# Folding w3 into w_out: multiplying each piece one step behind its transposes, and handing the steps out singly

## The chip, the cores and the metric

The kernel runs on one core of a Trainium2 chip. The metric is the device time of one execution in microseconds (us); of several runs the median counts. TensorE is PE in the profile (its weight loads PEld), VectorE is DVE, ScalarE is ACT, GpSimd is POOL, and SyncE, whose queue issues the DMAs, is SP.

## What is computed

```python
x = attention(q, k, v, M_prev, z_prev, beta)      # 2304 tokens x 512
h = x @ w_in                                      # 512 -> 2048
x2 = (h * tanh(softplus(h))) @ w_out              # 2048 -> 512
a, b = x2 @ w1, x2 @ w2                           # 512 -> 1024
out = ((a * b) @ w3) @ w_out2                     # 1024 -> 1024 -> 512
```

The inputs are 64-bit floats. The kernel decodes the weights from pairs of 32-bit words on the chip and multiplies in three terms (high x high, high x low, low x high). As nothing stands between the last two products, it computes W = w3 @ w_out2 once (the fold), and then out = (a * b) @ W.

## The kernel before

There are three stages in one program. **Stage one** is the attention (up to some 500 us). **Stage two** is the first feed-forward net. It goes through the quarters g = 0..3 of its 2048 hidden columns, and in each through eight units (b, z) of 288 tokens. `emit_h(u)` (L454) makes the hidden block: four PSUM tiles of 12 matmuls each, then tanh and friends on ScalarE and the splitting into gh and gl. `emit_x2(u)` (L560) multiplies it back and adds into x2 (L577, VectorE), in four rows of 12 matmuls; it is emitted one unit behind. **Stage three** (from L662) goes through 40 work items k = (c, m): five spans c of up to 512 tokens, eight blocks m of 128 hidden columns. `emit_ab(k)` (L699) makes two products of 12 matmuls and their product a * b, split into a ring of six; `emit_out(k - 5)` (L717) multiplies with W, five items behind.

**The fold** is a generator, `fold()` (L579), beside stage two's last quarter. It loads o2 (the split w_out2, 4 MB) into the memory that quarter 2's weights leave. Then, for each of the eight row blocks m and four column pieces g, a step loads 128 x 256 values of w3 (L92), decodes them (L98 to L104 on VectorE, L105 on GpSimd), transposes them in two halves into a PSUM tile (L597), copies the high part w3h out (L599, ScalarE), subtracts for the low part w3l (L600, by the helper of L65, VectorE), and multiplies: six matmuls into the accumulator `po`. After four pieces the row block leaves in two halves: ScalarE copy, VectorE subtraction, a store of 256 KB to w_dram (L611 to L613), with one buffer `wo`. There are 32 steps.

Five steps at a time are drawn in each unit of the last quarter but the first, between `emit_h` and `emit_x2` (L644, L645); the calls in stage three (L739, L674) only take what is left, which is nothing by then. W is loaded back (`wft`) in `end_fold()` (L673), called after the fifth work item.

PSUM has eight banks in three groups: A (3), X (3) and F (2). In the last quarter `emit_h` takes three A and one X, `emit_x2` takes X, and F belongs to the fold, one bank for `po` and one for the transposed piece. In stage three the second product of every odd work item takes F, and so does the fourth output tile of a span.

The order on each engine isn't the order of the text: a planner (the option `schedule_with_timeline_sim`) goes through the program on times that it works out itself, and gives each engine the earliest-written instruction that is ready by these times and whose tile has a free buffer. The order that comes out is fixed; on the chip the engines only wait for each other's semaphores. All DMAs of this part are issued from SP.

Of the kernel before, what the change touches and what calls it, by code (L numbers as in the profile page):

```python
# [21 lines left out]
def fused_kernel(ctx: ExitStack, tc, q, k, v, M_prev, z_prev, beta, w_in, w_out, w1, w2, w3, w_out2, out):  # L22
# [29 lines left out]
    def psF():  # L52
        return bank("F")

    def f(ap):
        return ap.bitcast(F32)
# [51 lines left out]
    def words(w, r0, c0):  # L108
        return w[r0:r0 + 128, c0:c0 + dec["w"]].bitcast(I32)
# [341 lines left out]
    HU = {(0, 0, 0): "AXAX", (0, 0, 1): "FXFX"}  # L451
    gt = {}

    def emit_h(u):  # L454

        g, b, z = u
        t = wts[g]
        x = xl[b]
        cs = slice(CH * z, CH * z + CH)
        y = [wps[0].tile([128, 2, CH], F32, tag=f"y{i}", name="y", bufs=1) for i in range(2)]  # L460
        hp = []
        for m in range(KQ):
            o = bank(HU.get(u, HT[g == NQ - 1])[m])[:, 0:CH]
            ms = slice(128 * m, 128 * m + 128)
            for kk in range(KD):
                mm(o, t[:, 0, kk, ms], x[:, 0, kk, cs], kk == 0, False)
                mm(o, t[:, 0, kk, ms], x[:, 1, kk, cs], False, False)
                mm(o, t[:, 1, kk, ms], x[:, 0, kk, cs], False, kk == KD - 1)
            hp.append(o)
        for m in range(KQ):  # L470
            nc.scalar.activation(out=y[m // 2][:, m % 2], in_=hp[m], func=AF.Tanh, scale=0.5)

        d = wps[0].tile([128, 1], F32, tag="dum", name="dum", bufs=2)
        first = nc.scalar.activation(out=d, in_=y[1][:, 1, 0:1], func=AF.Sin, scale=0.0)
        with tc.issue_after(first.ins):
            for i in range(2):
                nc.scalar.activation(out=y[i], in_=y[i], func=AF.Arctan, scale=-0.5, bias=half)
        gg = []
        for i in range(2):
            nc.scalar.activation(out=y[i], in_=y[i], func=AF.Sin, scale=-2.0, bias=halfpi)  # L480
            for j in range(2):
                nc.vector.tensor_tensor(out=y[i][:, j], in0=y[i][:, j], in1=hp[2 * i + j], op=ALU.mult)  # L482
            gh = wps[0].tile([128, 2, CH], F32R, tag="gh", name="gh", bufs=3)
            gl = wps[0].tile([128, 2, CH], F32R, tag="gl", name="gl", bufs=3)
            nc.scalar.copy(out=gh, in_=y[i])  # L485
            sub(gl, y[i], gh)
            gg.append((gh, gl))
        gt[u] = gg
# [68 lines left out]
    fk = ExitStack()  # L557
    fpool = [None]

    def emit_x2(u):  # L560
        g, b, z = u
        t = wts[g]
        gg = gt.pop(u)
        c0 = S * b + CH * z
        for m in range(KD):
            o = psX()[:, 0:CH]
            ms = slice(128 * m, 128 * m + 128)
            for kk in range(KQ):
                gh, gl = (x[:, kk % 2] for x in gg[kk // 2])
                mm(o, t[:, 0, KD + kk, ms], gh, kk == 0, False)  # L570
                mm(o, t[:, 1, KD + kk, ms], gh, False, False)
                mm(o, t[:, 0, KD + kk, ms], gl, False, kk == KQ - 1)
            d = x2[:, m, c0:c0 + CH]
            if g == 0:
                nc.vector.tensor_copy(out=d, in_=o)  # L575
            else:
                nc.vector.tensor_tensor(out=d, in0=d, in1=o, op=ALU.add)  # L577

    def fold():  # L579
        o2 = wq.tile([128, 2, 8, DM], F32R, tag="wq0", name="o2")  # L580
        oh, ol = o2[:, 0], o2[:, 1]
        for h in range(2):
            for i in range(2):
                dm(
                    out=f(o2[:, i, 4 * h:4 * h + 4]),
                    in_=o2_dram[i, 512 * h:512 * h + 512].rearrange("(k p) f -> p k f", p=128),
                )
        for m in range(FF2 // 128):
            po = psF()
            fp = fpool[0]  # L590
            for g in range(4):
                a, e = decode(words(w3, 128 * m, 256 * g))
                th = fp.tile([128, 2, 128], F32R, tag="w3h", name="w3h", bufs=2)
                tl = fp.tile([128, 2, 128], F32R, tag="w3l", name="w3l", bufs=2)
                pt = psF()[:, 0:256]
                for j in range(2):
                    nc.tensor.transpose(pt[:, 128 * j:128 * j + 128], a[:, 128 * j:128 * j + 128], ident)  # L597
                pw = pt.rearrange("p (a b) -> p a b", b=128)
                nc.scalar.copy(out=th, in_=pw)  # L599
                sub(tl, pw, th)  # L600
                for j in range(2):
                    kk = 2 * g + j
                    mm(po, th[:, j], oh[:, kk], kk == 0, False)
                    mm(po, th[:, j], ol[:, kk], False, False)
                    mm(po, tl[:, j], oh[:, kk], False, kk == 7)
                if g < 3:
                    yield
            for h in range(2):
                cs = slice(256 * h, 256 * h + 256)
                wo = fp.tile([128, 2, 256], F32R, tag="wo", name="wo", bufs=1)  # L610
                nc.scalar.copy(out=wo[:, 0], in_=po[:, cs])  # L611
                sub(wo[:, 1], po[:, cs], wo[:, 0])
                dm(out=w_dram[:, 128 * m:128 * m + 128, cs].rearrange("i p c -> p i c"), in_=f(wo))  # L613
            yield

    def from_dram(t, d, cols):
# [4 lines left out]
        return xp.tile([128, 2, KD, 512], F32R, tag=f"xs{s}", name=name, padded_shape=[128, 2, KD, S])  # L621

    folding = fold()
    nextq = iter(())
    prev = None
    w1t, w2t = [None, None], [None, None]
    for u in [(g, b, z) for g in range(NQ) for b in range(B) for z in range(2)]:
        g, b, z = u
        last = g == NQ - 1
        if u not in gt:  # L630
            if last and fpool[0] is None:
                steps(nextq, 100)
                steps(pre, 100)
                dk.close()
                fpool[0] = fk.enter_context(tc.tile_pool(name="fp", bufs=1))
                decoder(fk, 3, 2, 256)
            emit_h(u)
        if last:
            if z == 0 and b > 0:
                wt, wd = ((w1t, w1_dram), (w2t, w2_dram))[(b - 1) % 2]  # L640
                i = (b - 1) // 2
                wt[i] = w_slot(b - 1, "w12t")
                from_dram(wt[i], wd, slice(512 * i, 512 * i + 512))
            if (b, z) > (0, 0):  # L644
                steps(folding, 5)  # L645
        if prev is not None:
            emit_x2(prev)
        if not last:
            if b == 0 and z == 0:
                nextq = load_quarter(g + 1)  # L650
            steps(nextq, 2)
            steps(pre, 1)
        prev = u
    emit_x2(prev)
    w2t[1] = w_slot(3, "w12t")
    from_dram(w2t[1], w2_dram, slice(512, 1024))
    wk.close()
# [3 lines left out]

    wp3 = ctx.enter_context(tc.tile_pool(name="wp3", bufs=1, side="right"))  # L662
    T = 512
    NM = FF2 // 128
    RING = 6
    wft = [None]

    room = w2q[0].tile([128, 2 * RING + KD, T], F32R, tag="wq1", name="room")
    ring = room[:, 0:2 * RING].rearrange("p (r i) t -> p r i t", i=2)

    xs_ = {0: (wp3.tile([128, KD, T], F32R, name="x2h"), room[:, 2 * RING:])}

    def end_fold():  # L673
        steps(folding, 100)  # L674
        fk.close()
        late = ctx.enter_context(tc.tile_pool(name="late", bufs=1))
        x = late.tile([128, 2, KD, T], F32R, name="x2s")
        xs_[1] = (x[:, 0], x[:, 1])
        wft[0] = wq.tile([128, 2, NM, DM], F32R, tag="wq0", name="wft")
        for s in range(2):  # L680
            for i in range(2):
                dm(
                    out=f(wft[0][:, i, 4 * s:4 * s + 4]),
                    in_=w_dram[i, 512 * s:512 * s + 512, :].rearrange("(k p) f -> p k f", p=128),
                )

    spans = [(t, min(T, NT - t)) for t in range(0, NT, T)]
    work = [(c, m) for c in range(len(spans)) for m in range(NM)]
# [28 lines left out]
    def emit_out(k):  # L717

        c, m = work[k]
        t0, n = spans[c]  # L720
        t = ring[:, k % RING]
        if m == 0:
            outs[c] = [bank(tag) for tag in "XXXF"[0:n // 128]]
        for i, o in enumerate(outs[c]):
            ts = slice(128 * i, 128 * i + 128)
            mm(o, t[:, 0, ts], wft[0][:, 0, m], m == 0, False)
            mm(o, t[:, 0, ts], wft[0][:, 1, m], False, False)
            mm(o, t[:, 1, ts], wft[0][:, 0, m], False, m == NM - 1)
            if m == NM - 1:
                ob = wp3.tile([128, DM], F32, tag="ob", name="ob", bufs=2)  # L730
                nc.scalar.copy(out=ob, in_=o)
                dm(out=out[t0 + 128 * i:t0 + 128 * i + 128, :], in_=ob)
# [2 lines left out]
    split_x2(0)  # L735
    for k, (c, m) in enumerate(work):
        emit_ab(k)
        if k < LAG:
            steps(folding, 1)  # L739
        if k == LAG - 1:  # L740
            end_fold()
        if m == 5 and c + 1 < len(spans):
            split_x2(c + 1)
        if k >= LAG:
            emit_out(k - LAG)
# [34 lines left out]
```

## Time and profile before

| | us |
|---|---|
| median of 3 runs | 1074.87 (1072.59 to 1078.11) |
| profiled execution | 1077.63 |
| its span, first to last instruction | 1075.8 |
| PE busy | 1018.0 (95%) |
| VectorE busy | 678.0 (63%) |
| ScalarE busy | 540.9 (50%) |
| GpSimd busy | 392.7 (37%) |
| mean granted PE clock | 0.989 |

All times within the execution are us from the start of its span. A group of instructions is named by its line, engine, operation, output and inputs. Idle time stands with what ended it. A matmul's slice overlaps the next one's, and its end is modelled, so that starts say more than lengths.

### The profile page before, as it was taken

How to read it: one execution, taken by the hardware profiler on the slowest of the kernel's cores; microseconds unless marked ns; L12 is line 12 of the kernel's file. 1: busy time of each engine (PE TensorE's matmuls, PEld its weight loads, DVE VectorE, ACT ScalarE, POOL GpSimd, SP SyncE). 2: the span in 40 equal slices, each digit the busy share in tenths (PEclk: the TensorE clock that was granted, in tenths of full speed). 3: DMA queues.
4: the chain of work that ended last, by engine and by line, in shares of the span. 5: the costliest groups of instructions: out<-in, count | busy, mean ns of one | idle time of the engine just before them, and what ended most of it. 6: DMA issues, size and time to landing. Idle time of an engine off the chain costs nothing.

```text
span 1075.8 us, 17622 instructions
## 1 busy us (share of the span) xinstructions
PE 1018.0 (95%) x6360; PEld 874.8 (81%) x6360; DVE 678.0 (63%) x1630; ACT 540.9 (50%) x1128; POOL 392.7 (37%) x393
## 2 busy tenths in 40 slices
PE   6898898889998999999999999999889999999998
PEld 5665656567798999999999999998668888888897
DVE  6599999896689788988887456666543212121111
ACT  5675767577766566666666565643132122221212
POOL 7568898784255456555655011111100000000000
PEclk9999999999999999999999999999999999999999
DMA  6688777775233343334332174334232010100101
GB/s 148 166 188 190 179 185 177 168 187 124 79 88 99 108 143 133 104 120 150 111 106 98 51 274 149 124 94 144 68 121 76 1 40 1 40 1 1 40 1 59
DMA packets 115687, 116.60 MB, mean 108 GB/s; under 512 B 71952, under 2 KB 78096, under 8 KB 115600
## 3 DMA queue, kind: packets, MB, share of 16 engines
q1 hardware_dynamic: 115600, 115.48, 37.8%
q8 instruction: 50, 0.82, 0.3%
q14 instruction: 37, 0.30, 0.1%
HBM read 71.83 MB, written 21.50 MB: 87 GB/s over the span
## 4 chain that ended last, share of the span: by engine, by line
PE 61%; DVE 18%; DMA 7%; POOL 7%; issue 4%; SPq 1%; ACT 1%; DVEq 0%; POOLq 0%; ACTq 0%
PE psA L59 23%; PE psX L59 21%; PE psF L59 12%; DVE de L104 3%; POOL da L120 2%; PE psF L426 2%; DVE da L102 2%; DMA w_dram<-da 2%; DVE de L103 2%; POOL da L105 2%; DVE da L99 2%; DVE da L98 2%; DVE s L361 1%; DVE da L100 1%; PE psX L262 1%
## 5 line engine op out<-in xcount | busy, mean ns | idle before, releaser
L105 POOL TENSOR_TENSOR da<-da,de 128x512 f32<-128x512 f32 (+1 forms) x88 | 105.3, 1200 | 315.5 <-DVE de L104 287.9
L59 PE MATMUL psX<-gh,wqt 128*128 128x288 f32 x1024 | 209.8, 298 | 10.6 <-DVE x L575 6.1
L59 PEld LDWEIGHTS psX<-gh,wqt 128*128 128x128 f32 x1024 | 164.6, 188 | 13.9 <-DVE x L575 7.3
L59 PE MATMUL psX<-gl,wqt 128*128 128x288 f32 x512 | 151.5, 296 | 0.0
L59 PE MATMUL psA<-xt,wqt 128*128 128x288 f32 x840 | 122.6, 298 | 0.0
L59 PEld LDWEIGHTS psA<-xt,wqt 128*128 128x128 f32 x840 | 116.5, 191 | 2.2 <-issue 1.0
L366 ACT ACTIVATE s<-s,acc 128x512 f32<-128x512 f32 (+4 forms) x144 | 84.2, 587 | 40.0 <-DVE acc L361 34.3
L98 DVE TENSOR_SCALAR da<-draw 128x512 int32<-128x512 int32 (+1 forms) x88 | 46.6, 532 | 81.8 <-PE psF L597 31.1
L59 PEld LDWEIGHTS psX<-gl,wqt 128*128 128x128 f32 x512 | 96.8, 189 | 0.4
L712 ACT COPY bs<-psA 128x512 f32<-128x512 f32 (+1 forms) x40 | 21.8, 544 | 123.4 <-PE psA L59 118.5
L59 PE MATMUL psX<-wft,room 128*128 128x512 f32 x336 | 82.4, 390 | 0.0
L59 PE MATMUL psA<-x2h,w12t 128*128 128x512 f32 (+1 forms) x288 | 80.2, 355 | 0.5 <-ACT x2h L696 0.5
L426 PE MATMUL psF<-ident,s 128*128 128x128 f32 x400 | 68.1, 284 | 10.8 <-DVE s L356 7.2
L59 PE MATMUL psF<-xt,wqt 128*128 128x288 f32 x552 | 77.3, 295 | 0.0
L59 PEld LDWEIGHTS psF<-xt,wqt 128*128 128x128 f32 x552 | 74.5, 188 | 0.1
L59 PE MATMUL psX<-pt,raw 128*64 128x64 f32 (+4 forms) x576 | 74.1, 328 | 0.0
L361 DVE CUSTOM_DVE_ANT_0 s<-psA,mask 128x512 f32<-128x512 f32 (+3 forms) x144 | 64.2, 478 | 15.2 <-PE psA L59 11.4
L59 PEld LDWEIGHTS psX<-wft,room 128*128 128x128 f32 x336 | 62.6, 188 | 12.6
L485 ACT CAST gh<-y 128x576 fp32r<-128x576 f32 x64 | 43.2, 675 | 56.0 <-DVE y L482 40.2
L713 DVE TENSOR_TENSOR bs<-bs,psA 128x512 f32<-128x512 f32 (+1 forms) x20 | 12.7, 634 | 93.1 <-PE psA L59 92.4
L428 ACT COPY pt<-psF 128x512 f32<-128x512 f32 (+1 forms) x112 | 57.2, 541 | 26.0 <-PE psF L426 25.7
L426 PEld LDWEIGHTS psF<-ident,s 128*128 128x128 f32 x400 | 48.0, 145 | 27.3 <-issue 7.1
(130 smaller groups left out, 2219.0 us busy)
## 6 DMA issues: line engine op xcount, KB each, us to landing
draw<-in_moe_w_out_dram SPq DMA_DIRECT2D x24, 512.0 KB, 3.7
draw<-in_moe_w_in_dram SPq DMA_DIRECT2D x16, 512.0 KB, 4.4
draw<-in_moe_w_dram SPq DMA_DIRECT2D x16, 512.0 KB, 4.1
draw<-in_moe_w_dram SPq DMA_DIRECT2D x32, 256.0 KB, 3.0
w12t<-w_dram SPq DMA_DIRECT2D x8, 1024.0 KB, 7.3
out_dram<-ob SPq DMA_DIRECT2D x18, 256.0 KB, 2.0
eqk<-hl SPq DMA_DIRECT2D x30, 144.0 KB, 2.6
eqk<-hk SPq DMA_DIRECT2D x30, 144.0 KB, 2.7
```

The costliest lines, as they stand in the source:

```text
L59: nc.tensor.matmul(o, lhsT=l, rhs=r, start=start, stop=stop)
L98: V.tensor_scalar(out=ai, in0=hw, scalar1=0x7FFFFFFF, scalar2=None, op0=ALU.bitwise_and)
L99: V.tensor_scalar(out=a, in0=a, scalar1=2.0 ** -15, scalar2=122879.9921875, op0=ALU.max, op1=ALU.min)
L102: V.scalar_tensor_tensor(out=ai, in0=hw, scalar=-0x40000000, in1=ai, op0=ALU.bitwise_and, op1=ALU.bitwise_or)
L104: V.scalar_tensor_tensor(out=e, in0=lw.bitcast(U32), scalar=2.0 ** -52, in1=e, op0=ALU.mult, op1=ALU.mult)
L105: nc.gpsimd.tensor_tensor(out=a, in0=a, in1=e, op=ALU.add)
L361: nc.vector.tensor_tensor_reduce(out=s, in0=o, in1=m, op0=ALU.add, op1=ALU.min, scale=-scale, scalar=init, accum_out=a,)
L366: nc.scalar.activation(out=s, in_=s, func=AF.Exp, scale=-1.0, bias=a, accum_out=r)
L426: nc.tensor.transpose(o[:, 128 * x:128 * x + 128], src[:, 128 * jb:128 * jb + 128], ident)
L428: nc.scalar.copy(out=t[:, 0:n], in_=o[:, 0:n])
L485: nc.scalar.copy(out=gh, in_=y[i])
L712: nc.scalar.copy(out=bs, in_=pb)
```

## The change

The fold's loop becomes one loop over 33 steps: step s decodes, transposes and splits piece s, and then multiplies piece s - 1, kept in `held`; `po` is taken when the multiplication of a row's first piece is emitted. The steps are drawn one at a time: one after the second of `emit_h`'s four tiles, one after each of `emit_x2`'s four rows, in the same units as before. What `end_fold()` did (drawing the rest, closing the fold's pool, opening the pool with x2s, loading `wft`) stands ahead of the last `emit_x2`, and the calls within stage three go.

```diff
@@ emit_h
+            if m in (1,):
+                steps(beside, 1)
@@ emit_x2
                 nc.vector.tensor_tensor(out=d, in0=d, in1=o, op=ALU.add)
+            steps(beside, 1)
@@ fold
-        for m in range(FF2 // 128):
-            po = psF()
-            fp = fpool[0]
-            for g in range(4):
-                a, e = decode(words(w3, 128 * m, 256 * g))
+        held = None
+        po = None
+        fp = fpool[0]
+        for s in range(4 * (FF2 // 128) + 1):
+            piece = None
+            if s < 4 * (FF2 // 128):
+                a, e = decode(words(w3, 128 * (s // 4), 256 * (s % 4)))
                 ...
                 nc.scalar.copy(out=th, in_=pw)
                 sub(tl, pw, th)
+                piece = (s, th, tl)
+            if held is not None:
+                n, th, tl = held
+                m, g = n // 4, n % 4
+                if g == 0:
+                    po = psF()
                 for j in range(2):
                     kk = 2 * g + j
                     mm(po, th[:, j], oh[:, kk], kk == 0, False)
                     mm(po, th[:, j], ol[:, kk], False, False)
                     mm(po, tl[:, j], oh[:, kk], False, kk == 7)
-                if g < 3:
-                    yield
-            for h in range(2):
-                ...
+                if g == 3:
+                    for h in range(2):
+                        ...
+            held = piece
             yield
@@ stage two
-            emit_h(u)
+            emit_h(u, folding if last and (b, z) > (0, 0) else iter(()))
         ...
-            if (b, z) > (0, 0):
-                steps(folding, 5)
         if prev is not None:
-            emit_x2(prev)
+            emit_x2(prev, folding if last and (b, z) > (0, 0) else pre0)
         ...
-    emit_x2(prev)
+    NM = FF2 // 128
+
+    steps(folding, 100)
+    fk.close()
+    late = ctx.enter_context(tc.tile_pool(name="late", bufs=1))
+    x2s = late.tile([128, 2, KD, 512], F32R, name="x2s")
+    wft = wq.tile([128, 2, NM, DM], F32R, tag="wq0", name="wft")
+    for s in range(2):
+        for i in range(2):
+            dm(
+                out=f(wft[:, i, 4 * s:4 * s + 4]),
+                in_=w_dram[i, 512 * s:512 * s + 512, :].rearrange("(k p) f -> p k f", p=128),
+            )
+    emit_x2(prev, pre0)
     w2t[1] = w_slot(3, "w12t")
     from_dram(w2t[1], w2_dram, slice(512, 1024))
@@ stage three
-    def end_fold():
-        ...
         emit_ab(k)
-        if k < LAG:
-            steps(folding, 1)
-        if k == LAG - 1:
-            end_fold()
```

## Rows read from the trace of the kernel before

**Rows 1.** The page's engine lines: busy us, share of the span, instructions.
```profile
PE 1018.0 (95%) x6360; PEld 874.8 (81%) x6360; DVE 678.0 (63%) x1630; ACT 540.9 (50%) x1128; POOL 392.7 (37%) x393
```

**Rows 2.** Windows: stretch, length, busy us per engine (instructions), granted clock, DMA share, GB/s.
```profile
600.00:620.00 20.00, 19.93 (x139) 19.93 (x140) 9.92 (x26) 11.99 (x19) 1.19 (x2) 0.91 0.08 23
645.27:665.27 20.00, 20.00 (x140) 19.13 (x139) 13.74 (x40) 10.51 (x19) 2.20 (x3) 1.00 0.50 164
745.27:798.74 53.47, 44.96 (x187) 32.98 (x186) 29.75 (x80) 11.16 (x26) 6.84 (x9) 0.97 0.26 79
850.00:1000.00 150.00, 150.00 (x663) 124.24 (x662) 30.23 (x46) 31.75 (x55) 0.00 (x0) 1.00 0.04 16
```

**Rows 3.** Groups of PE by form, 745.5 to 798.7: count, busy us and mean ns, idle before.
```profile
L59 PE MATMUL psF<-o,w3h 128*128 128x512 f32 x44 | 15.5, 435 | 5.6 <-DVE w3l L65 2.8 <-ACT w3h L599 2.8
L59 PE MATMUL psA<-x2h,w12t 128*128 128x512 f32 x48 | 15.4, 396 | 0.5 <-ACT x2h L696 0.5
L59 PE MATMUL psF<-o,w3l 128*128 128x512 f32 x22 | 9.5, 433 | 0.6 <-DVE w3l L65 0.6
L59 PE MATMUL psA<-room,w12t 128*128 128x512 f32 x24 | 9.4, 392 | 0.0
L59 PE MATMUL psF<-x2h,w12t 128*128 128x512 f32 x16 | 5.4, 397 | 0.8 <-DVE bs L713 0.8
L597 PE MATMUL psF<-ident,da 128*128 128x128 f32 x22 | 4.5, 286 | 1.0 <-DVE wo L65 1.0
L59 PE MATMUL psF<-room,w12t 128*128 128x512 f32 x8 | 3.1, 392 | 0.0
```

**Rows 4.** The chain that ended last: start us, us, what (xinstructions).
```profile
745.47 0.63 ACT x2h L696
...
790.54 4.42 PE psF L59 x18
...
853.14 2.72 PE psA L59 x12
```

**Rows 5.** Timeline of PE: start us, us, instruction, count.
```profile
625.29 0.39 PE L59 MATMUL psF<-o,w3h 128*128 128x512 f32 x1
625.52 0.38 PE L597 MATMUL psF<-ident,da 128*128 128x128 f32 x2
...
679.81 0.38 PE L597 MATMUL psF<-ident,da 128*128 128x128 f32 x2
...
683.09 0.63 PE L59 MATMUL psF<-o,w3h 128*128 128x512 f32 x2
...
684.35 0.40 PE L59 MATMUL psF<-o,w3l 128*128 128x512 f32 x1
...
685.27 0.38 PE L597 MATMUL psF<-ident,da 128*128 128x128 f32 x2
685.41 0.38 PE L59 MATMUL psA<-xt,wqt 128*128 128x288 f32 x1
...
690.33 0.38 PE L597 MATMUL psF<-ident,da 128*128 128x128 f32 x2
...
697.39 0.38 PE L597 MATMUL psF<-ident,da 128*128 128x128 f32 x2
...
745.27 0.38 PE L597 MATMUL psF<-ident,da 128*128 128x128 f32 x2
746.14 0.74 PE L59 MATMUL psA<-x2h,w12t 128*128 128x512 f32 x2 [0.49 <-ACT x2h L696]
```

**Rows 6.** Timelines of ACT and DVE: the row leaving behind the transposes at 690.33.
```profile
690.53 0.37 ACT L611 CAST wo<-psF 128x256 fp32r<-128x256 f32 x1 [1.90 <-PE psF L59]
...
695.23 0.42 DVE L65 TENSOR_TENSOR wo<-psF,wo 128x256 fp32r<-128x256 f32 x1 [1.82 <-ACT wo L611]
```

**Rows 7.** Timelines of DVE and PE: a decode that waits, and PE behind it.
```profile
595.70 0.29 DVE L98 TENSOR_SCALAR da<-draw 128x256 int32<-128x256 int32 x1 [6.71 <-DMA draw<-in_moe_w_dram]
...
600.07 0.53 PE L59 MATMUL psX<-gh,wqt 128*128 128x288 f32 x2 [2.29 <-DVE x L577]
```

More of the change, by code (lines that the diff above doesn't have):

```diff
@@ L452, in fused_kernel, with emit_h @@
     gt = {}
-    def emit_h(u):
+    def emit_h(u, beside=iter(())):
         g, b, z = u
@@ L558, in fused_kernel, with emit_x2 @@
     fpool = [None]
-    def emit_x2(u):
+    def emit_x2(u, beside):
         g, b, z = u
@@ L605, in fold @@
                     mm(po, tl[:, j], oh[:, kk], False, kk == 7)
-                if g < 3:
-                    yield
-            for h in range(2):
[L609 to L613, printed above, removed]
+                if g == 3:
+                    for h in range(2):
+                        cs = slice(256 * h, 256 * h + 256)
+                        wo = fp.tile([128, 2, 256], F32R, tag="wo", name="wo", bufs=1)
+                        nc.scalar.copy(out=wo[:, 0], in_=po[:, cs])
+                        sub(wo[:, 1], po[:, cs], wo[:, 0])
+                        dm(out=w_dram[:, 128 * m:128 * m + 128, cs].rearrange("i p c -> p i c"), in_=f(wo))
+            held = piece
             yield
@@ L623, in fused_kernel @@
     folding = fold()
+    pre0 = iter(())
     nextq = iter(())
@@ L663, in fused_kernel @@
     T = 512
-    NM = FF2 // 128
     RING = 6
-    wft = [None]
     room = w2q[0].tile([128, 2 * RING + KD, T], F32R, tag="wq1", name="room")
     ring = room[:, 0:2 * RING].rearrange("p (r i) t -> p r i t", i=2)
-    xs_ = {0: (wp3.tile([128, KD, T], F32R, name="x2h"), room[:, 2 * RING:])}
-    def end_fold():
[L674 to L685, printed above, removed]
+    xs_ = {0: (wp3.tile([128, KD, T], F32R, name="x2h"), room[:, 2 * RING:]), 1: (x2s[:, 0], x2s[:, 1])}
     spans = [(t, min(T, NT - t)) for t in range(0, NT, T)]
@@ L725, in emit_out @@
             ts = slice(128 * i, 128 * i + 128)
-            mm(o, t[:, 0, ts], wft[0][:, 0, m], m == 0, False)
-            mm(o, t[:, 0, ts], wft[0][:, 1, m], False, False)
-            mm(o, t[:, 1, ts], wft[0][:, 0, m], False, m == NM - 1)
+            mm(o, t[:, 0, ts], wft[:, 0, m], m == 0, False)
+            mm(o, t[:, 0, ts], wft[:, 1, m], False, False)
+            mm(o, t[:, 1, ts], wft[:, 0, m], False, m == NM - 1)
             if m == NM - 1:
```

## The prediction

> **What bounds the kernel now.** First the page's engine line: TensorE (PE) is busy 95% of the span [rows 1], so only stretches where it does less can give time back. The windows show where [rows 2]: it is busy for all of 645.27 to 665.27, inside stage two's last quarter, and all of 850 to 1000, inside stage three; the stretch that falls short is 745.27 to 798.74, the seam between them, with 44.96 of 53.47 us. That figure flatters it, since a matmul's slice overlaps the next one's start. I count work instead. The instructions of the seam by form [rows 3] are 66 matmuls of the fold (44 + 22), 96 of stage three (48 + 24 + 16 + 8) and 22 transposes. In steady stage three 12 matmuls of 512 columns take 2.72 us on the chain [rows 4], 0.2267 each; a transpose pair moves the next matmul by 0.14 us (685.27 to 685.41 in the timeline [rows 5]). So the seam holds 162 x 0.2267 + 11 x 0.14 = 38.3 us of work, and **15.2 us of it are empty**, a little of it at the lower clock (granted 0.97 on average [rows 2]).
>
> Two measures of the empty time differ. By matmul slices it is 53.47 - 44.96 = 8.5 us; by count 15.2; by weight loads, busy 32.98 of 53.47 against 124.24 of 150 at full stream [rows 2], it is 53.47 - 32.98 x 150 / 124.24 = 13.7. I take the count. The Trainium skill (Perfetto Trace Analysis, Identifying the Most-Contended Engine) says that matmul busy share is no good measure of the distance to the limit and that the share of LDWEIGHTS is. The trace agrees, 13.7 lying near 15.2; by the slices alone the sum below would end at 1067, not 1061.
>
> Why the seam is empty is in the timeline of PE [rows 5]. A piece's two transposes (L597) are followed by a ScalarE copy, a VectorE subtraction, then six matmuls, and only then by the next piece's transposes: 679.81, matmuls from 683.09, first matmul with w3l at 684.35, next transposes 685.27. From the second piece (625.52) to the 22nd (745.27) there are 20 intervals, 5.99 us each. Inside a row block they are 5.1 to 5.5; each fourth is longer (690.33 to 697.39), because the two F banks hold the accumulator and one transposed piece, and the next piece waits until the finished row is out, through copy, subtraction, store, copy, subtraction (690.53 to 695.65 [rows 6]). F banks are taken in the order of their first write: the second piece's transposes come only behind the first multiplication (625.29, 625.52), which waited for o2. So when stage two ends 10 pairs of transposes and 11 multiplications remain, and the first work item of stage three whose second product goes to F (k = 1) stands behind all of them. Four halves of A work run meanwhile (72 matmuls), then PE has the fold's chain alone; k = 1 ends in the 18 matmuls from 790.54 [rows 4].
>
> **The change part by part.** Nothing is computed less: the same 64 transposes, 192 matmuls, 32 decodes, 32 loads and 16 stores.
>
> 1. *Multiply one step behind.* Transposes of piece s+1 now stand ahead of the six matmuls of piece s. They need the F bank of piece s, free once w3l is subtracted. The interval inside a row, 5.46 and 5.06 us in two cases (679.81, 685.27, 690.33 [rows 5]), loses the six matmuls, 6 x 0.2267 = 1.36 us: 4.1 and 3.7. From above it is bounded by 684.35 - 679.81 = 4.5, when w3l was used at the latest. I take 4.2, nearest to the middle of the three. At a row's end the next accumulator needs the old one's bank, but one more piece is transposed before it is needed. From a row's first transposes: the row before ends 1.5 us later, its bank is out 7 us after that (690.33 to 697.39, the planner's own spacing), one more piece follows at once, so two pieces take 9 us, then two at 4.2, and 1 us for the w3h buffer that waits for the late multiplication: about 18.5 us a row against 24 now.
>
> 2. *Where it ends.* The second piece no longer waits for o2, the third does, so at 625.5 the fold is one piece ahead. It is at the fourth piece near 631, at the fifth near 635, six rows later (6 x 18.5) at 746, and at the last near 760, its subtraction done near 764. Stage two meanwhile takes in the matmuls that stood behind it: 745.27 + 66 x 0.2267 + 11 x 0.14 = 761.8. So fold and stage two end together. If the fold is late, the 72 matmuls that need no F bank cover 16.3 us, until 778. Only a row of 20.5 us or more eats into the gain.
>
> 3. *Steps handed out singly.* No instruction more; it lowers a step's priority against the row blocks of `emit_x2`, and so keeps x2's additions from queueing behind five decodes. Zero, bounds -1 (the stall of [rows 7], gone) to the rival below. VectorE, busy 13.74 of 20 us with four pieces [rows 2], gets five in the 21 us of a longer unit: it covers them.
>
> 4. *W's transfer with the second stage's end.* Four issues on SP, waiting for the fold's last stores and o2's last reader. They start near 768; W is first needed by `emit_out(0)` behind six work items (6 x 24 x 0.2267 = 32.6 us after the start of stage three, near 795). Zero either way. Behind them on SP stands the last quarter of w2, needed by the fifth item, 21.8 us after stage three starts. It is read into a buffer free since the last `emit_h`, so the planner should issue it first; if it does not, it lands some us later and costs 0 to 5. I take 0. The late pool takes the fold pool's memory, as now.
>
> 5. *The seam that stays.* The first matmul of stage three waits for a cast of x2 into memory that stage two's last matmul frees: 745.27 to 746.14 [rows 5], the cast 0.63 [rows 4], so 0.87 us; bounds 0 (a late piece of the fold fills it) and 2.3, the x2 wait of [rows 7].
>
> Sum: four work items (96 x 0.2267 = 21.8 us) end at 761.8 + 0.9 + 21.8 = 784.5, where before it was 798.74. **Gain 14.2 us**, bounds 11 and 15.2; I round to 13.9, for the last unit has a thinner cover. The profiled execution took 1077.63 (span 1075.8): 1063.7 by the sum. The median of the runs shown is 1074.87, 2.8 lower, so I forecast **1061.0**.
>
> **Rivals.** *The interval hardly shrinks.* Decoding, a busy ScalarE or the row-end store sets the pace, say 21.5 us a row: the last transposes come near 635 + 6 x 21.5 + 16 = 780, the F bank 4 us later, some 6 us behind the cover: about 1067 to 1069. For: a row's end already costs 7 us and ScalarE has table loads in its way. Against: inside a row transposes follow the multiplication directly, so the decoded words were there. Chance 0.11.
>
> *Nothing moves.* The planner still puts each multiplication first, because both become ready with the same subtraction, and row ends get no shorter: the fold ends where it did, 1073 to 1076. Against: program order favours the transposes now, and planner and trace follow it for F banks. Chance 0.06.
>
> *VectorE blocks PE.* At 595.70 a decode had waited 6.71 us for its load, x2's addition stood behind it, and PE idled 2.29 us [rows 7]; the 20 us that follow ran at a granted 0.91 [rows 2], another 1.8 us. That is 4.1 us. With five pieces a unit and additions between them it could happen in each of the seven units with steps: 28.7 us; from four on (16.4) it eats the gain, at five or six the kernel takes about 1081. The Trainium skill (PSUM — Partial Sum Buffer, Engine vs sequencer instructions) says that VectorE's queue is strictly first in, first out, which speaks for this rival: a decode that waits holds the additions behind it. The trace shows it that once. Against: in 645.27 to 665.27 PE did not idle with four pieces [rows 2], and the three load buffers stay. Chance 0.07.
>
> **How the numbers follow.** Main case 0.76, first rival 0.11, second 0.06, third 0.07. About 0.5% (5.4 us) is what a measurement of this kernel can tell from no change. Faster by more than that: all of the main case and 0.07 of the first rival, 0.83; within: the rest of it, the second rival and a mild third, 0.11; slower: 0.06. The main case alone spans 1057.5 (gain 15.2, and 2 us by which medians of three differ here) to 1065; with the first rival the range goes to 1069.
>
> **What would show it.** Right: transposes ahead of the previous piece's multiplication, rows of the fold about 18.5 us apart, the last transposes near 760, PE without a hole between 746 and 800, the clock at 1.00 there, the first F product of stage three within 10 us of its start, W issued near 768. Wrong: intervals still near 6 us, or x2 additions that wait on loads. A fold that is early and a time that is not would mean that the empty 15 us were needed by something behind.

## The result and the profile after

The changed kernel takes **1059.26 us** (median of 4 runs, 1057.27 to 1062.18) beside 1076.09 of the kernel before in the same comparison (1072.59 to 1078.11): ratio 0.9849, 95% interval 0.9812 to 0.9887. Forecast were 1061.0 us, faster, from 1057.5 to 1069. The profiled execution took 1062.18 us (span 1060.4), 15.4 less than the one before.

Two executions are not equally far on when they come to the stretch that was changed. The first decode of the fold began at 593.75 here and at 595.70 before [rows 7], and the two programs do the same up to there. So times of after are compared with times of before less 1.95, and the change itself is worth 15.4 - 1.95 = 13.5 us of these two executions.

The page's engine line answers to [rows 1]. The instructions of PE are the same, its weight loads take 877.0 us instead of 874.8, and the span is 15.4 shorter:

```profile
PE 1014.3 (96%) x6360; PEld 877.0 (83%) x6360; DVE 675.2 (64%) x1630; ACT 541.6 (51%) x1128; POOL 389.9 (37%) x393
```

Windows of after, columns as in [rows 2]. The third is the stretch of the seam of before, 745.27 to 798.74, set 1.95 earlier:

```profile
600.00:620.00 20.00, 20.00 (x143) 20.00 (x143) 9.63 (x27) 11.83 (x20) 0.00 (x0) 0.92 0.12 33
640.00:660.00 20.00, 20.00 (x136) 18.89 (x135) 15.42 (x45) 11.50 (x23) 3.07 (x4) 1.00 0.34 90
743.33:796.79 53.46, 53.46 (x268) 45.63 (x267) 26.27 (x58) 15.35 (x30) 2.96 (x4) 1.00 0.34 115
850.00:1000.00 150.00, 150.00 (x664) 124.21 (x663) 30.03 (x46) 32.92 (x57) 0.00 (x0) 1.00 0.06 22
```

The hole is gone: PE is busy for all of the 53.46 us, with weight loads for 45.63 of them where it was 32.98, and the granted clock is 1.00, where it was 0.97. Stage three (850 to 1000) has not changed, and neither has the lower clock behind the idle time ahead of the fold (600 to 620).

What PE does in that third stretch, by form (columns as in [rows 3]):

```profile
L59 PE MATMUL psA<-x2h,w12t 128*128 128x512 f32 x73 | 23.2, 391 | 0.0
...
L59 PE MATMUL psX<-gh,wqt 128*128 128x288 f32 x43 | 8.9, 297 | 0.0
...
L59 PE MATMUL psF<-o,w3h 128*128 128x512 f32 x24 | 7.8, 399 | 0.0
...
L603 PE MATMUL psF<-ident,da 128*128 128x128 f32 x10 | 1.9, 271 | 0.0
...
```

The idle column, which held 8.5 us in sum before [rows 3], is 0.0 in these and in the seven rows left out. Counted as in the prediction the eleven rows are 193 matmuls of 512 columns at 0.2267 (43.8 us), 65 of 288 columns at 0.133 (28 in 3.72 us, first row of the chain below: 8.6) and 5 transpose pairs at 0.14 (0.7): 53.1 us of work in 53.46, where it was 38.3. The same stretch of time holds 14.8 us more of work.

The new order, in the chain of waits of after (start us, us, what), from the end of stage two to the fifth work item:

```profile
735.05 3.72 PE psX L59 x28
...
753.71 1.58 PE psX L59 x12
755.30 2.85 PE psF L59 x12
...
764.98 0.22 PE psF L603 x2
...
768.17 4.08 PE psF L59 x18
...
783.13 8.16 PE psA L59 x36
```

Stage two's last matmuls (psX, 753.71) are followed by two multiplications of the fold, and stage three begins at 758.13 with one pair of transposes (764.98) and two multiplications of the fold still to come; before, there were ten pairs and eleven multiplications. The 18 matmuls in F that came at 790.54 [rows 4] come at 768.17.

### The profile page after: what moved, and what is told of

Read it like the earlier page. It is cut to its first block, busy times and chain, and to the rows that moved or that the text cites. A ratio compares the mean times of both kernels' runs of the same rounds, so it can differ in the third digit from the quotient of the medians.

```text
span 1060.4 us, 17637 instructions
## 1 busy us (share of the span) xinstructions
PE 1014.3 (96%) x6360; PEld 877.0 (83%) x6360; DVE 675.2 (64%) x1630; ACT 541.6 (51%) x1128; POOL 389.9 (37%) x393
## 4 chain that ended last, share of the span: by engine, by line
PE 60%; DVE 20%; POOL 8%; DMA 6%; issue 4%; SPq 2%; ACT 0%; POOLq 0%; DVEq 0%
PE psA L59 24%; PE psX L59 20%; PE psF L59 12%; DVE de L104 3%; POOL da L120 2%; DMA w_dram<-da 2%; DVE da L102 2%; DVE s L361 2%; POOL da L105 2%; DVE de L103 2%; PE psF L426 2%; DVE da L98 2%; DVE da L99 2%; DVE da L100 2%; DVE s L356 1%
## 5 line engine op out<-in xcount | busy, mean ns | idle before, releaser
L105 POOL TENSOR_TENSOR da<-da,de 128x512 f32<-128x512 f32 (+1 forms) x88 | 103.0, 1174 | 292.7 <-DVE de L104 270.4
L98 DVE TENSOR_SCALAR da<-draw 128x512 int32<-128x512 int32 (+1 forms) x88 | 48.4, 553 | 68.7 <-POOL wqt L65 19.1
```

The source lines that it names most:

```text
L98: V.tensor_scalar(out=ai, in0=hw, scalar1=0x7FFFFFFF, scalar2=None, op0=ALU.bitwise_and)
L105: nc.gpsimd.tensor_tensor(out=a, in0=a, in1=e, op=ALU.add)
```

## The experiments

My theory: PE's empty time came from the fold's end falling behind stage two's, and the new loop, with the transposes ahead of the previous multiplication, shortens the fold; the single steps and W's early transfer are worth nothing. The rivals: the single steps or W's transfer bring a part of it, or the idle time ahead of the fold [rows 7] has a part in it. "Before" and "after" name the kernel that an experiment starts from. Ratios are to the kernel before on the same chip, with 95% intervals.

**The three parts, each alone.** Before with the new loop of the fold only (five steps at a time, W loaded as before):

```diff
-            for g in range(4):
-                a, e = decode(words(w3, 128 * m, 256 * g))
+        for s in range(4 * (FF2 // 128) + 1):
...
+            if held is not None:
+                n, th, tl = held
...
+            held = piece
```

> Only the fold's loop with the multiplication one step behind; steps drawn five at a time, W loaded after the fifth work item as before. Theory (the place of the transposes ahead of the multiplication, and the F bank that it frees, are the whole change): the fold's rows about 19 us apart as in the changed kernel, PE without a hole between 746 and 800, gain 13 to 16 us, ratio 0.985 to 0.988. Rival (handing out singly keeps additions of x2 from queueing behind five decodes and is needed): half of the gain or less, ratio 0.992 to 1, PE waiting for x2 additions in stage two.

Measured: 1059.67 us, 0.9871 (0.9841 to 0.9902). PE's timeline at the end of stage two (columns as in [rows 5]):

```profile
754.79 0.38 PE L600 MATMUL psF<-ident,da 128*128 128x128 f32 x2
754.93 0.48 PE L59 MATMUL psF<-o,w3h 128*128 128x512 f32 x1
...
755.47 0.86 PE L59 MATMUL psA<-x2h,w12t 128*128 128x512 f32 x3
```

The transposes (L600 here) stand within the multiplication of the piece before them, and stage three starts at 755.47 without a gap. The loop alone gives the whole gain that can be measured.

Before with the single steps only:

```diff
+            if m in (1,):
+                steps(beside, 1)
...
+            steps(beside, 1)
...
-                steps(folding, 5)
```

> Only the handing out: the fold's old loop (a piece's multiplication ahead of the next transposes), its steps drawn singly behind the second tile of emit_h and the rows of emit_x2. Theory: the fold stays at 6 us a piece, some ten pieces are left when stage two ends, the hole in the seam stays at 15 us: ratio 0.998 to 1.002. Rival (the single steps carry the gain): ratio 0.985 to 0.993.

Measured: 1074.76 us, 1.001 (0.9989 to 1.003). The old seam is there, in the chain:

```profile
789.95 4.41 PE psF L59 x18
```

Before with only the pool's end and W's transfer ahead of the last `emit_x2`:

```diff
+    steps(folding, 100)
+    fk.close()
...
     emit_x2(prev)
...
-        if k == LAG - 1:
-            end_fold()
```

> Only the end: the pool closed and W's load written ahead of the last emit_x2, the fold's loop and its handing out as before. Theory: W waits for the fold's last stores wherever it is written, so its load starts near 790 as before, and nothing moves: ratio 0.998 to 1.002. Rival (the early load carries part of the gain, or holds up the last quarter of w2 behind it on SP): ratio 0.993 to 0.997, or above 1.003 with work items waiting for w12t.

Measured: 1075.28 us, 1.0012 (0.9993 to 1.0032). SP's timeline:

```profile
784.39 0.91 SPq L663 DMA_DIRECT2D wft<-w_dram  x2
785.40 10.03 SPq L613 DMA_DIRECT2D w_dram<-wo  x2
797.32 0.91 SPq L663 DMA_DIRECT2D wft<-w_dram  x2
```

An order in the text that lets W go early doesn't make it go early. Its first half, which holds the row blocks that were stored long before, is issued at 784.39, when the fold's last matmul ends (783.97, 0.40 us long): W comes into the memory of o2, and this matmul is o2's last reader. Only the second half waits for the fold's last stores. Both rivals of this kind fall.

**Is it the bank F, or the fold's end itself?** The prediction named the first F product of stage three as the thing that waits. Before, with the first five work items using A banks only:

```diff
-        pb, pa = (bank(t)[:, 0:n] for t in ("AA", "AF")[m % 2])
+        pb, pa = (bank(t)[:, 0:n] for t in ("AA", "AF")[m % 2 if k >= 5 else 0])
```

> The kernel before with the first five work items of stage three taking both products from the A banks, so that none of them stands behind the fold for an F bank. Theory (the hole is PE work that is there but has no bank): items 1, 3 and 4 run while the fold goes on, the hole shrinks and a smaller one appears later, where the first emit_out waits for W: gain 4 to 10 us, ratio 0.990 to 0.996. Rival (the fold's own chain bounds the seam, whoever waits): gain under 2 us, ratio 0.998 to 1.

Measured: 1074.1 us, 0.9997 (0.9978 to 1.0015). This was a miss for the theory: no gain at all, as the rival had it. The windows, the chain and one of PE's waits of this kernel say where it went:

```profile
765.00:800.00 35.00, 31.53 (x136) 24.59 (x135) 16.31 (x46) 5.76 (x14) 4.38 (x6) 0.95 0.16 52
800.00:820.00 20.00, 14.40 (x52) 10.77 (x51) 6.15 (x11) 5.60 (x11) 0.00 (x0) 0.83 0.52 181
```

```profile
790.78 2.41 DMA w_dram<-wo
...
801.25 1.68 PE psF L59 x6
802.95 0.36 SPq L682
...
803.35 8.58 DMA wft<-w_dram
```

```profile
PE psX L59 <- DMA wft<-w_dram: 5.1, 2, 3.1
```

The work items went on without F, and PE had no idle time from 740.36 to 790. But their matmuls now stood between those of the fold, which ended at 802.93, behind them and some 15 us later than in before (791.81 and the 0.39 of that matmul, with the first decode at 595.70 there and 591.41 here). The hole moved and came in two parts. From 790.04 the fold's chain ran alone again: three pairs of transposes and three multiplications, 4.5 us of work by the count, took until 802.93, behind a store of 2.41 us (790.78). Then `emit_out(0)` waited for W: issued at 802.95, landed 8.58 us after 803.35, 5.1 us of idle PE. The granted clock of 800 to 820 was 0.83. So F was only the first of two things that stand behind the fold's end, with W right behind it. Giving the first another resource shifts the wait; an earlier end of the fold serves both.

**How early must the fold end?** After, with its steps begun one unit later, and two units later:

```diff
-            emit_h(u, folding if last and (b, z) > (0, 0) else iter(()))
+            emit_h(u, folding if last and (b, z) > (0, 1) else iter(()))
...
-            emit_x2(prev, folding if last and (b, z) > (0, 0) else pre0)
+            emit_x2(prev, folding if last and (b, z) > (0, 1) else pre0)
```

(the second with `(1, 0)`), beside the changed kernel itself on the same chip:

> The changed kernel itself, beside the three that follow on the same chip. Every theory: ratio 0.985 to 0.988.

> The changed kernel with its steps begun one unit later, 31 drawn singly and the rest together at the end of stage two. Theory (lateness costs only what goes beyond the cover of 72 matmuls without an F bank): some five pieces are left at the seam, their last subtraction comes about 3 us after the cover ends: 1 to 5 us more than the changed kernel, ratio 0.987 to 0.991. Rival (every piece left over costs its own 1.4 us a piece or more): 7 us or more, 0.992 or above.

> The changed kernel with its steps begun two units later. Theory: about nine pieces are left at the seam, the cover of 16 us ends with some three pieces still to come, each about 2.7 us when PE has nothing else: 8 to 11 us more than the changed kernel, ratio 0.993 to 0.997. Rival (the cover is not what matters, and the order of transposes and multiplications makes the gain wherever the fold ends): within 3 us of the changed kernel.

Measured: after 1062.53 us, 0.9889 (0.9863 to 0.9915); one unit late 1061.55, 0.9887 (0.9862 to 0.9912); two units late 1068.37, 0.995 (0.9932 to 0.9967), 5.8 us more than after. PE's timelines of the two: the first matmul of stage three, the last transposes, the first F product of stage three. One unit late:

```profile
748.00 0.86 PE L59 MATMUL psA<-x2h,w12t 128*128 128x512 f32 x3
...
771.24 0.38 PE L603 MATMUL psF<-ident,da 128*128 128x128 f32 x2
...
773.78 0.39 PE L59 MATMUL psF<-x2h,w12t 128*128 128x512 f32 x1
```

Two units late:

```profile
746.85 0.86 PE L59 MATMUL psA<-x2h,w12t 128*128 128x512 f32 x3
...
775.44 0.41 PE L603 MATMUL psF<-ident,da 128*128 128x128 f32 x2 [2.09 <-DVE w3l L65]
...
783.08 0.39 PE L603 MATMUL psF<-ident,da 128*128 128x128 f32 x2
...
785.59 0.39 PE L59 MATMUL psF<-x2h,w12t 128*128 128x512 f32 x1
```

The same lines of after:

```profile
758.13 0.94 PE L59 MATMUL psA<-x2h,w12t 128*128 128x512 f32 x3
...
764.82 0.38 PE L603 MATMUL psF<-ident,da 128*128 128x128 f32 x2
...
769.37 0.39 PE L59 MATMUL psF<-x2h,w12t 128*128 128x512 f32 x1
```

And the first F product of before, where stage three starts at 746.14 [rows 5]:

```profile
792.04 0.39 PE L59 MATMUL psF<-x2h,w12t 128*128 128x512 f32 x1
```

In after the first F product comes at 769.37, 11.2 us behind the start of stage three (758.13), and the last transposes at 764.82. One unit late it comes 25.8 us behind the start. Five pairs of transposes and six multiplications of the fold were left there; with the 72 matmuls that need no F bank they are 108 x 0.2267 + 5 x 0.14 = 25.2 us of work, so the wait is filled. Two units late it comes 38.7 us behind, and nine pairs, ten multiplications and the 72 matmuls make 132 x 0.2267 + 9 x 0.14 = 31.2: 7.5 us empty by this count, 5.8 measured in the time. In before it is 45.9 (746.14 to 792.04) with ten pairs, eleven multiplications and the 72 matmuls, 32.7 us of work. So a fold that begins a whole unit (some 21 us of stage two) late still ends in time; I had expected it to cost 1 to 5 us, and for two units 8 to 11 (the ratio of the second, 0.995, lies in the range given for it).

**Is it the row's end that paces the fold?** Two units late, with two buffers `wo` instead of one (paid with one of the three buffers for w3's loads):

```diff
-                        wo = fp.tile([128, 2, 256], F32R, tag="wo", name="wo", bufs=1)
+                        wo = fp.tile([128, 2, 256], F32R, tag="wo", name="wo", bufs=2)
...
-                decoder(fk, 3, 2, 256)
+                decoder(fk, 2, 2, 256)
```

> The changed kernel with its steps begun two units later, as in d2_units_late, and with a second buffer for the row that leaves (for it, two load buffers for w3 instead of three). Theory of the prediction (a row's end, through copy, subtraction, store, copy, subtraction, holds the F bank and costs the fold most of what a row takes beyond 4.2 us a piece): rows of the fold near 17 us instead of 18.4 to 19, the loss against the changed kernel 0 to 3 us instead of 6, ratio 0.988 to 0.992. Rival (inside a row the chain transposes, copy, subtraction takes near 5 us, and the row's end is hidden behind it): rows and time as in d2_units_late, ratio 0.993 to 0.997.

Measured: 1063.71 us, 0.9907 (0.9887 to 0.9928), against 0.995 (0.9932 to 0.9967) with one buffer; the intervals don't meet. PE's timeline, the first transposes of three rows running:

```profile
678.53 0.38 PE L603 MATMUL psF<-ident,da 128*128 128x128 f32 x2
...
696.73 0.38 PE L603 MATMUL psF<-ident,da 128*128 128x128 f32 x2
...
714.96 0.38 PE L603 MATMUL psF<-ident,da 128*128 128x128 f32 x2
...
733.68 0.38 PE L603 MATMUL psF<-ident,da 128*128 128x128 f32 x2
```

Rows of 18.2, 18.2 and 18.7 us; with one buffer the same rows (from 684.08, 702.48 and 721.53 to 740.84) took 18.4, 19.1 and 19.3. That is 1.6 us over three rows, so the row's end still holds the fold a little; the time came as the theory had it, but the rows of 17 us did not. Stage three starts at 743.27 here, and its first F product comes 34.1 us behind that, where it was 38.7:

```profile
777.38 0.39 PE L59 MATMUL psF<-x2h,w12t 128*128 128x512 f32 x1
```

These 4.6 us are the gain of 4.7 in the time. Eight pairs and nine multiplications are left at the start of stage three instead of nine and ten (1.5 us of work less), and by the count 4.4 us are empty instead of 7.5. So the larger part, 3.1 us, is empty time that is gone from the seam. It matters only where the fold is late.

**The idle time ahead of the fold.** It is in after as it was before. Timelines of VectorE and PE, answering to [rows 7]:

```profile
593.75 0.30 DVE L98 TENSOR_SCALAR da<-draw 128x256 int32<-128x256 int32 x1 [6.67 <-DMA draw<-in_moe_w_dram]
...
598.13 0.53 PE L59 MATMUL psX<-gh,wqt 128*128 128x288 f32 x2 [2.26 <-DVE x L579]
```

After and before, each with the first two decodes put behind the additions to x2 of the unit at hand (the edit of after; in before the condition is `(m, g) < (0, 2)`):

```diff
-                nc.vector.tensor_tensor(out=d, in0=d, in1=o, op=ALU.add)
+                added[u] = nc.vector.tensor_tensor(out=d, in0=d, in1=o, op=ALU.add)
...
-                a, e = decode(words(w3, 128 * (s // 4), 256 * (s % 4)))
+                with tc.issue_after(added[2, 3, 0].ins) if s < 2 else ExitStack():
+                    a, e = decode(words(w3, 128 * (s // 4), 256 * (s % 4)))
```

> The changed kernel with the first two decodes of the fold placed on VectorE behind the x2 additions of unit (2, 3, 0), so that they no longer hold these up while they wait for their load. Theory (the only hole left beside the fold is that wait: 2.29 us of idle PE and then some 20 us at a granted clock of 0.91 to 0.92): 4 us less than the changed kernel, ratio to the kernel before 0.981 to 0.984, PE without idle between 590 and 603. Rival (the first pieces come later, the fold ends later and its cover runs out, or the idle time only moves): no less than the changed kernel, 0.985 to 0.99.

> The kernel before with only the first two decodes placed behind the x2 additions of unit (2, 3, 0). Theory (the wait ahead of the fold and the hole at the seam are separate holes on the same chain): the 2.3 us of idle PE and what the clock loses go, the seam stays: 2 to 4 us less, ratio 0.996 to 0.998. Rival (the fold, late as it is, eats what is won ahead of it): 1.000.

Measured: with after 1057.46 us, 0.9851 (0.9826 to 0.9876), 5.1 under after on the same chip (the ratio misses the 0.981 to 0.984 of the theory, as after itself stood at 0.9889 there); with before 1069.7, 0.9959 (0.9944 to 0.9974), a gain of 0.41% or 4.4 us beside the 4.1 that the prediction worked out for this stall. Windows of before with its decodes behind (b2):

```profile
590.00:602.00 12.00, 12.00 (x93) 12.00 (x92) 7.21 (x22) 8.12 (x13) 0.01 (x1) 1.00 0.22 68
765.00:800.00 35.00, 27.77 (x115) 19.74 (x116) 19.83 (x49) 8.89 (x21) 4.31 (x6) 1.00 0.37 121
```

PE is busy throughout 590 to 602, and the seam is as empty as ever: from the first matmul of stage three to the first with W it takes 51.9 us (740.32 to 792.23), in before 52.4 (746.14 to 798.58). The stall ahead of the fold and the seam are two separate losses; the change took only the second.

The first of these kernels beats the change, so it was run again, beside after:

> The changed kernel with the first two decodes behind the x2 additions, once more, beside the changed kernel. Theory: 2 to 5 us less than the changed kernel. Rival: within 1 us of it.

> The changed kernel once more, beside the three others. Every theory: ratio 0.985 to 0.989.

Measured: 1058.49 us, 0.9852 (0.9827 to 0.9878), and after 1059.7, 0.9867 (0.9846 to 0.9888). The advantage is 1.2 us here and 5.1 above, and the intervals of the ratios overlap in both. Both comparisons together, ten runs of each kernel, have means of 1058.2 and 1061.3 us: 3.1 us, give or take some 2. So the best version is after with the decodes behind, by an amount that is not settled.

## Why the prediction was right, step by step

**What bounds the kernel.** Right. The count of empty time, 15.2 us, is borne out: the like stretch holds 14.8 us more of work. The other measure by weight loads had said 13.7, the slices 8.5. The stretch itself gained 13.7 (the four work items end at 783.13, with the fold done before them; before at 798.74, less the 1.95).

The Trainium skill (Perfetto Trace Analysis, Identifying the Most-Contended Engine) holds the share of LDWEIGHTS to be the better measure of the distance to the limit than matmul busy time. The trace agrees: 13.7 by it and 13.7 gained, while the slices showed 8.5; that the two are the same number is partly chance, as the count is 14.8 to 15.2. And the full stream that the share is measured against has to be one of the same matmuls. The stretch of after holds 65 matmuls of 288 columns, and by stage three's 124.21 of 150 its empty time would be 53.46 - 45.63 x 150 / 124.21 = -1.6 us.

**Step 1, the interval.** The row was nearly right, as a sum of two errors. Timeline of after, all engines, from the third transposes of a row on:

```profile
682.43 0.38 PE L603 MATMUL psF<-ident,da 128*128 128x128 f32 x2
...
684.04 0.36 ACT L605 CAST w3h<-psF 128x256 fp32r<-128x256 f32 x1
...
685.09 0.41 DVE L65 TENSOR_TENSOR w3l<-psF,w3h 128x256 fp32r<-128x256 f32 x1
...
686.17 0.63 PE L59 MATMUL psF<-o,w3h 128*128 128x512 f32 x2
...
687.43 0.38 PE L603 MATMUL psF<-ident,da 128*128 128x128 f32 x2
...
692.38 0.38 PE L603 MATMUL psF<-ident,da 128*128 128x128 f32 x2
```

Inside a row I took 4.2 us; it is 5.00 and 4.95. The bank is free at 685.50, when the subtraction ends, but the transposes stand behind two matmuls of the previous piece and some of stage two, 1.9 us later: the six matmuls that I struck out of the interval did not all leave it. PE waits for nothing in these rows (its one wait is shown below), so the order on PE, which the planner made, sets this interval, and not the bank. The two pieces at the row's end were given 9 us and took 9.23 (673.20 to 682.43). The 1 us for the buffer of w3h does not show. Sum 19.18 for this row, 19.07 on average (635.50 to 749.93, six rows), where I said 18.5. One reading ahead of the sum was too narrow: the intervals inside a row of before are not 5.1 to 5.5 us but 4.81 (675.00 to 679.81) to 6.13 (731.97 to 738.10); the sum took its own two, 5.46 and 5.06.

**Step 2, the end.** Right in kind, 5 to 7 us too early in place. The fourth and fifth pieces came at 631.04 and 635.50, or 633.0 and 637.5 with the 1.95 added (near 631 and 635 forecast). The last transposes came at 764.82, or 766.8, instead of near 760: some 2.5 us of it were there at the fifth piece, and the six rows added 3.4. The first F product came 11.2 us behind the start of stage three, where within 10 was the sign. It cost nothing, since the cover of 72 matmuls, forecast to last until 778, is there: of the two experiments with a later start, it holds in the one (25.8 us to the first F product, 25.2 of work) and fails in the other (38.7 and 31.2). Stage three's four items were forecast to end at 784.5; they ended at 783.13, or 785.1 with the 1.95 added.

**Step 3, steps singly.** Zero, and measured as 1.001 alone. VectorE's cover was there: 15.42 busy of 20 us in 640 to 660, and no wait of PE for it. (The 20 us of before that the step goes by hold three decodes, not four, so that its argument was weaker than it read.)

**Step 4, W.** Zero, and 1.0012 alone. SP's timeline of after:

```profile
736.14 0.38 SPq L630 DMA_DIRECT2D w12t<-w_dram  x1
...
769.57 0.94 SPq L674 DMA_DIRECT2D wft<-w_dram  x2
```

W's first half was issued at 769.57, as the fold's last matmul ended, or 771.5 with the 1.95 added (near 768 forecast), and w2's last quarter long before it, at 736.14, as the step had chosen between its two cases.

**Step 5, the seam that stays.** Forecast 0.87, measured 0: 12 matmuls of the fold stand between stage two and 758.13, the lower bound's own reason (a late piece of the fold fills it).

**The sum.** 14.2 forecast for the stretch, 13.7 measured in it. The median came out 1.7 below the forecast; the interval of the ratio alone is 8 us wide, so that difference has no cause to look for.

**The rivals.** The interval did shrink, and the row ends with it. That nothing moves is refuted by the 31 pairs of transposes that stand ahead of stage three. VectorE blocks PE once, ahead of the fold, as before, and never in the units with steps; these are PE's waits in after from 588 to 800, all of them:

```profile
PE psX L59 <- DVE x L579: 2.3, 1, 2.3
```

The Trainium skill (PSUM — Partial Sum Buffer, Engine vs sequencer instructions) has VectorE work strictly in order. The trace agrees for that one place, and putting the two decodes behind the additions took its 2.26 us away. That five pieces a unit would bring more such places was not borne out.

**What the prediction had only half.** Its account of the wait, that the F product of stage three is held by F, is true of the kernel before and is not the whole cause: without that wait the time stayed the same, since the fold's own chain and then W took its place.

## What to carry to other kernels

In a software pipeline over few accumulators, put the next piece's preparation ahead of the previous piece's multiplication: the buffer it needs is free once the previous piece was copied out, before that has been multiplied. Before giving a waiting instruction another buffer, look for who else waits for the same late producer; if there is a second one soon behind, only an earlier producer helps. And measure how late the producer may be: here a whole unit of delay cost nothing that could be measured, so a still shorter fold is not likely to bring anything.

## What was not expected

An idle PE of nearly the same length was followed by different clocks. Behind 2.26 us (after) and 2.29 (before) the granted clock of 600 to 620 was 0.92 and 0.91. Behind 2.29 us with the new loop alone and 2.21 with the later start it fell too. Behind 2.27 us with the single steps alone, 2.24 with the two buffers `wo`, and 1.66 to 1.88 us in five other executions it stayed at 1.00. The windows with the new loop alone (the stall ends at 595.43) and with the single steps alone (it ends at 601.03):

```profile
590.00:602.00 12.00, 9.71 (x62) 9.47 (x61) 8.08 (x22) 6.01 (x10) 1.51 (x2) 0.86 0.28 89
```

```profile
600.00:620.00 20.00, 18.97 (x143) 18.97 (x144) 11.41 (x29) 12.03 (x19) 1.47 (x2) 1.00 0.13 33
```

Where it fell, it was 0.50, the lower of its two levels, for some 3 us that began 1 to 2 us behind the stall, with PE at work again (in after from 600.13 to 602.13 throughout), and 5 us behind the stall it was 1.00 again. In the 5 us behind the stall PE began 26 matmuls in these four executions and 38 in the others: 12 of 0.133 us, 1.6 us lost. So the price of that stall is about 2 us in some executions and 4 in others. Whether that is why the advantage of removing it came out as 5.1 and as 1.2 was not shown; the two executions of after that were profiled in these comparisons don't speak for it, since the clock stayed at 1.00 in both (1.66 and 1.82 us).

The first decode of the fold, up to which the programs do the same, began anywhere from 589.34 us (W's early transfer alone) to 596.69 (two units late) in the executions profiled here, leaving out the kernels that move it; in three executions of the changed kernel itself it was 592.25, 593.75 and 596.17. A single profile can't tell a change of some microseconds from this, unless its times are set against such a common point.
